# W2's loads and the remainders of W1 and W3 from GpSimd's queue, and a new order of TensorE's steps

## The chip, the cores and the metric

The kernel runs on one core of one Trainium2 chip. Its time is the device time of one execution in microseconds (us); what is told is the median of several runs. Beside it stands one execution taken by the hardware profiler, whose span (first to last instruction) and whose engines' work the profile shows.

## The reference

Two transformer layers over one sequence of 2048 positions with width 576. A layer adds memory-augmented attention on its layer norm, and then a gated feed-forward on its layer norm. Both layers use the same weights. In bf16, with 32 heads of 128, segments of 32 positions, 8 memory rows and F = 4608:

```python
for s in range(64):                                # segments, one after the other
    h = concatenate([mem, x[:, 32*s:32*s+32]])     # 8 + 32 rows of width 576
    q, k, v = h @ Wq, h @ Wk, h @ Wv               # 32 heads of 128
    p = softmax(where(mask, q @ k.T * 128**-0.5, -1e9))
    o = (p @ v) @ Wo                               # summed over the heads
    mem = o[:, :8]                                 # handed to the next segment
    outs.append(o[:, 8:])

h = silu(x @ w1) * (x @ w3)                        # 2048 x 4608
out = h @ w2

x = x + A(layernorm(x)); x = x + B(layernorm(x))   # layer 1
x = x + A(layernorm(x)); x = x + B(layernorm(x))   # layer 2
```

The memory makes the attention of a layer a chain of 64 segments. A segment of layer 2 can run as soon as layer 1 has left its group of four segments behind.

## The kernel before

**Steps.** The work goes in steps. Step t handles segment t of layer 1 and segment t-8 of layer 2 at once (`LAG = 8`), so most steps have both layers in one matmul of 80 columns: 40 rows of each. There are 72 steps; the first and last 8 have one layer alone. In a step TensorE does, by nodes of the program: `QK` and `QKt` (queries and keys of four heads, eight units; the first works on the 512 leading rows of width 576, the second on the 64-row remainder), `SC` (scores, four groups of eight heads), `PV` (P times V), `WO` and `WOt` (the output projection), and the `V` products. Softmax runs on VectorE and ScalarE: five steps on VectorE and an exponential. In steps of both layers P is transposed by a DMA, `TRD`, that reads the one buffer `PB` and writes one of two buffers `PTS`; in steps of one layer TensorE does it (`TR`).

**Feed-forward.** For each group of four segments and both layers a job runs beside the steps: layer norm (`F...`: statistics on VectorE, the reciprocal root `pow` on GpSimd, the norm on VectorE, transposes on TensorE), then 18 pairs of F blocks of 128. A pair takes W1 and W3 for 256 of the F columns and W2 for 256 of the F rows. `FF` multiplies the 512 leading rows, `FFt` the 64-row remainder, tanh and two products make the gated hidden values, and `W2` and `W2b` (one for each layer) multiply two pairs' worth by W2. The weights don't stay: every pair is loaded anew for every job.

**Buffers.** Two buffers hold W1 and W3 of a pair (pool `w13`, tile `W13`), two hold W2 (pool `w2`, tile `W2C`). So the loads of a pair wait until the pair two before has been read. A pair's load is five DMAs, all on SyncE's queue: two blocks of 128 x 4 x 256 (W1 and W3), two remainders of 64 x 256, and W2 as 128 x 2 x 576:

```python
for kind, wd in ((0, self.a.w1), (1, self.a.w3)):
    self.dma(W[:, 4 * kind:4 * kind + 4], wd[0:4 * P, fa:fa + 2 * P].rearrange("(c p) f -> p c f", p=P))
for kind, wd in ((0, self.a.w1), (1, self.a.w3)):
    self.dma(W[kind * R64:(kind + 1) * R64, 8], wd[4 * P:D, fa:fa + 2 * P])
```

**Order.** A planner places every node in the program's order. TensorE's order is not the planner's choice: it is written out by hand or by a search as a string with one letter for each TensorE node (`ORDER`: `FIRST`, then `FOUR` eleven times, then `LAST`). One `FOUR` is a round of 16 steps. The letters that matter here: Q and q are `QK` and `QKt`, S is `SC`, P is `PV`, O and o the output projection, F and f are `FF` and `FFt`, W and w are `W2` and `W2b`, a, b, m and n transposes. The other engines and the queues get their instructions in the order of the planned starts, computed from a table of durations, and each engine then works strictly in that order; waits on semaphores follow from what is read and written. Where one instruction waits, all behind it on its engine's queue wait too.

**SyncE's queue** carries the weights of the start, the five loads of each pair, the x tiles for layer 1's first norm, and the transpositions. **GpSimd's queue** carries the residual x (`XR`), the stores, the `pow` of each norm, and in each step a zeroing of `PB`, which waits until the last transposition of the step before has read it.

In the profile nearly all matmuls have line L626, VectorE's operations L632, ScalarE's L629, loads from SyncE L635, loads and stores from GpSimd L641, transpositions L1049, zeroings L1046 and `pow` L795. `W<-in_B_w_dram` are W1 and W3 (256 KB the blocks, 32 KB the remainders); the `W` in `bank<-XTB,W` is the same tile, the one in `bank<-HT,W` the weights of queries and keys.

One thing in the start depends on the order: the main part of a unit, `qk`, writes 12 matmuls of freshly loaded W against the identity ahead of units 0 and 4 of step 0, but only if it is the first to touch its banks:

```python
first = self.begin(b)
for c in range(4 if first and t == 0 and u % 4 == 0 else 0):
    for _ in range(3):
        self.mm(self.bk(b[1])[:], self.T.ident[:, 0:P], self.T.W[:, 4 + c, u * 512:(u + 1) * 512], True, True)
```

Of the kernel before, what the change touches and what calls it, by code (L numbers as in the profile page):

```python
# [199 lines left out]
def ewh(*ns):  # L200
# [2 lines left out]


FIRST = (
    "amQqQqSqQTqQQqSqQqSQqQTSvVXxPPTOPOTOoooPOoQQqqqqQSQQSvqVqQQSqTQqXPSTOPTOaooPxTOPoOoQQqqQSQqqVvSQTqqqQQSQqPSTPOOT"
    "PTOPoooOoQqqqqQQSQVvSqQQqqqQSQTPTSXPOTxOTPooPOOooQpQqqvVqqSQnQQFSqfqQQTSfqqFPQFTSOfoPWTFPOTOPfooOoFfqqQQQSFfqvVq"
    "qQWSQFQqqqfQQSTWPSFffXTFPxOTWFTfPOPOOooooFfqqQQFSQfVqqqvQWSQFffqFQTQSPWTQqfqOPSFTOPFWTOPooffOooFQQqqqqQSWQvVfSFQ"
    "qQTqWaSQPqqQTOSPboXTOPoTOPxxOooXQpqqqQQSvnQfqQSFqqQVSFffQFPqqQfFSPWOFoPfOoOofWPFOoFfqqQQQSWqqqQQQqfSFSGqgqQQFfgP"
    "GSWPFGFffggGOPOWPOOooooFfqqQQWSfqqFQQvFSVqqfQQFqfSQWQqfPaSfFPOOPWOFFPfoooOoWQqqqqQQbSQGqqgSQQQqSPGgqQOSPGOgGPgOP"  # L210
    "oooOoQqqqppQQQvSqqVnnSQFqfqQQFPSqffFQPWOSwFFPffOOwPWOooooFffqqQFQQwQSWFqfqFSGqqgfQQQPQSWFqqfgGSGPwGggOPOOPwOoooo"
    "WFqffFQQQwQqqqWSaSFqfqqQQQvSVffqFQFPPwOWSofFOFPwWffFPOOoooWQqqqQQSqqqbQQQSwGSgqqgQQPGSggGPGOPOOPoooOo"
)
FOUR = (
    "QqqqppQvVSQQnnQFfqqFSfqqQQFfqQSWPwPSFffOOWPFOFPwOooooFqffqQQQQqgqWSwGSFfqqQQQPQSWFqfqfFSGwgggGPGOPOPOOWooooFqqff"
    "QQFQQqqvwSSFfqqVQwQWFPSFffqqQQPOWSwFFPffOOWPwOooooFfqqQQqqaSQQWqqSQqqQQQbSwGSggGPGggPGOPOOPoooOo"
)
LAST = (
    "QqqppQQSQvqqqVSQQnqqnQSFPfqfQOoPSFOFPWfOFPwOoooFffqqQQQQfqqWSSwFfqqFQQwQWQqqSFffggGFPGWSwPFggfGGPOOPwOOoWoooFqfq"
    "qQQQSFqfqQQvSVqqfFQQQqfSPWwSOPFFOPWwffFPOOoWwoooFQQqfqFSqfqQQQSqqWQvVSqqQQVSPPbwXvxOPOOPoooOoQQppvqqVqqQSQQqqnnQ"  # L220
    "SFfqFTSQQPTfqfFPSWOOwFTffFTPWPOOooowoFfqvVqqQQQwQSFqqqfQSQWTSFfqfqQFQwPSTWPFTffFPOTOPOOoooowxvXVqqQQQqqQWSSFQffq"
    "qQFSQTwFTfqqQPWTSOFPFPTOfPOOoooowWqqQQQSQqqfvVSwFWffFTQPqqQWqqSQTQPOSwbOTXPxooTOPoOoQqqpQQSVqqvQQQSqqqnSQqTQFPST"
    "fOPFTOPofoTOPwOfooFVfqqvQQFSQFqqqfQQSQqqqQQSTwPTFSPOOfxooTXfPTFPOOooFQfqqqQQSVvqqwQQFSfqTQqqQSQPwTSOPFffTOFPwTOP"
    "oofOooFVvqqqQQQqSqqQQSQwQTqqSQPTSOFPFfoOTTofPPOOoopwFFffnFFwfffFFwffFfFwwwfffFFFFwffFFwffFFwffFFwfffFFww"
)
ORDER = FIRST + FOUR * 11 + LAST

# [8 lines left out]
def make_nodes(em, nseg, pools, o=Opt, dma_bw=230e3, load_bw=400e3):  # L236
# [34 lines left out]
    b = banks(1)  # L271
# [190 lines left out]
                 prio=prio, mode="full/col", acq=b, name="POST")  # L462
        return node("DVE", dve(576), em.post_add(li, g, xr[g], b[0]), deps=[d], prio=prio, rel=b, name="POSTa")

    last_up = []
    last_reads = [], []
    kept = {}

    def job(j):

        ents = [(0, j)] if 0 <= j < ngrp else []
# [6 lines left out]
        last = s0 >= nst  # L478
        wr = []
# [26 lines left out]
        for at, pp in enumerate([npp - 1] + list(range(npp - 1)) if last else range(split, npp)):  # L506
            mids, w2s, htts, lds = [], [], [], []
            stays = last and pp == npp - 1
            ents = own + [(1, own[0][1] - 1)] if last and pp == 0 else own
            ne = len(ents)  # L510
            mm = (128 * ne / 2.4 + 2.5) / 1000
            for pr_ in (2 * pp, 2 * pp + 1):
                prio = s0 + o.ff + (o.win if s0 + 4 < nst else o.last_win) * (2 * at + pr_ % 2) / NPR
                if stays:
                    w13, w2 = kept[pr_]
                    ld = []
                    w2s.append(w2)
                elif last:
                    w13 = w2 = None
                    ld = tail[pp]  # L520
                else:
                    keep = s0 < nst <= s0 + 4 and pp == npp - 1
                    w13, w2 = Slot("w13", users=2 + keep), Slot("w2", users=ne + keep)
                    kept[pr_] = w13, w2
                    ld = [node("DMA", kb(1152, 256) / dma_bw, em.load_w13(pr_, w13), prio=prio - 1, acq=[w13], lat=2.0, name="W13")]
                    lds.append(node("DMA", kb(256, 576) / dma_bw, em.load_w2(pr_, w2), prio=prio - 0.99, acq=[w2], lat=2.0, name="W2l"))
                    w2s.append(w2)
                b = banks()
                htt = Slot("htt", users=ne)
# [46 lines left out]
    for t in range(nst):  # L576
        if t % 4 == 2 and (t + 2) // 4 < ngrp:
            x_in((t + 2) // 4)
        if t == LAG:
            ht_mem[t].append(node("DVE", 0.1, em.init_mem(1, LAG), deps=[m0e] + reads_ht.get(LAG - R_HT, []), prio=LAG - 2, name="m0"))  # L580
        if role(t) == 0 or t == 0:
            vx_pair(t - role(t), t - 1 + o.vx)
        step(t)
        if t % 4 == 1 and t // 4 < ngrp:
            x_res(t // 4)
        if t % 4 == 3:
            job((t + 1) // 4 - 1)
        elif t == nst - 1:
            job(nst // 4)
# [13 lines left out]
class Emitter:  # L603
# [788 lines left out]
```

## Time and profile before

| | |
|---|---|
| median of 3 runs | 2653.09 us (2650.92 to 2656.6) |
| the profiled execution | 2660.77 us |
| its span | 2659.0 us |
| granted TensorE clock | 0.995 |
| TensorE busy | 2570.4 us (97%) |
| VectorE, ScalarE, GpSimd busy | 2019.7, 1263.2, 129.8 us |
| HBM read | 306.72 MB |

PE is TensorE's matmuls, PEld its weight loads, which run beside them; DVE is VectorE, ACT ScalarE, POOL GpSimd, SP SyncE. A q behind the name is the queue of an engine, where DMAs are issued. A group's row gives the line, engine, operation, what is written from what, the count, then the busy time, the mean in ns, and the idle time before it with what ended it. A row of waits gives who waited for whom: us in total, times, longest. A row of DMA issues gives the size and the median time from issue to landing. A row of windows gives, for a stretch, the busy time of each engine, the granted clock, the DMA engines' share and GB/s. A row of the timeline gives start, duration, engine, line and what was done.

### The profile page before, as it was taken

Reading aid. Unit: us, or ns where it says so; the run is one execution under the profiler, and the core shown is the slowest. Engines: PE = TensorE matmul, PEld = TensorE weight load, DVE = VectorE, ACT = ScalarE, POOL = GpSimd, SP = SyncE. Lnnn points to the kernel's source line nnn. Section 1 sums busy time; section 2 is a strip of 40 time slices with the busy share of each in tenths; the row PEclk is TensorE's granted clock in tenths of the full one; section 3 lists DMA queues with packets and bytes.
Section 4 is the critical chain, followed back from the end, with each engine's and each line's share of the span. In section 5 each row is a group of like instructions: output and inputs, shape, how many; then the busy total and the mean of one; then the engine's idle time right before and its main releaser. Section 6 shows DMA issues by size and latency. Waiting matters only on the chain.

```text
span 2659.0 us, 131834 instructions
## 1 busy us (share of the span) xinstructions
PE 2570.4 (97%) x58597; PEld 2216.3 (83%) x58626; DVE 2019.7 (76%) x5188; ACT 1263.2 (48%) x3694; POOL 129.8 (5%) x182
## 2 busy tenths in 40 slices
PE   6999999999999999999999999999999999999998
PEld 4787888888888888888888888888888888888886
DVE  4777776877787778778777877877777777778876
ACT  2655553544445454444545444454544445454552
POOL 1000000000000000000000000000000000000000
PEclk9999999999999999999999999999999999999999
DMA  9065745465565556556555645545465454645357
GB/s 322 8 187 129 186 101 142 122 147 137 125 144 115 145 119 157 131 126 142 113 145 118 156 131 130 147 111 140 117 157 140 122 148 101 151 114 146 108 162 240
DMA packets 683196, 371.39 MB, mean 140 GB/s; under 512 B 233752, under 2 KB 672800, under 8 KB 681984
## 3 DMA queue, kind: packets, MB, share of 16 engines
q1 hardware_dynamic: 678944, 355.00, 52.4%
q8 instruction: 458, 7.50, 1.2%
q0 software_dynamic: 3024, 6.93, 0.9%
q10 hardware_dynamic: 656, 1.02, 0.2%
q14 instruction: 114, 0.93, 0.1%
HBM read 306.72 MB, written 2.36 MB: 116 GB/s over the span
## 4 chain that ended last, share of the span: by engine, by line
PE 83%; DMA 10%; DVE 4%; issue 2%; SPq 1%; ACT 1%; POOL 0%; ACTq 0%; DVEq 0%; POOLq 0%
PE bank L626 83%; DMA PTS<-PB 6%; DMA W<-in_B_w_dram 3%; DVE PB L632 1%; SPq L635 1%; DVE SME L632 1%; DMA W<-in_A_Wk_dram 1%; DVE STAT L632 1%; DVE HTT L632 1%; DMA WO<-in_A_Wo_dram 0%; DVE V L632 0%; DMA XN<-in_A_x_dram 0%; DVE XR L632 0%; ACT HT L629 0%; ACT HTT L629 0%
## 5 line engine op out<-in xcount | busy, mean ns | idle before, releaser
L626 PEld LDWEIGHTS <-W 128*128 128x128 bf16 (+2 forms) x32200 | 1261.3, 100 | 137.2 <-issue 68.9
L626 PE MATMUL bank<-HT,W 128*128 128x80 bf16 (+3 forms) x23040 | 798.1, 197 | 13.6 <-issue 6.5
L626 PE MATMUL bank<-XTB,W 128*64 128x256 bf16 (+5 forms) x9160 | 660.5, 263 | 14.5 <-DMA W<-in_B_w_dram 11.1
L629 ACT ACTIVATE QKT<-bank 128x64 bf16<-128x64 f32 (+2 forms) x1640 | 379.5, 309 | 301.8 <-PE bank L626 269.6
L626 PE MATMUL bank<-OT,WO 128*128 128x80 bf16 (+3 forms) x11520 | 403.0, 198 | 3.3 <-issue 1.6
L626 PEld LDWEIGHTS <-WO 128*128 128x128 bf16 (+1 forms) x11520 | 377.1, 102 | 29.6 <-issue 13.1
L629 ACT ACTIVATE V<-bank 32x512 bf16<-32x512 f32 (+1 forms) x586 | 331.8, 585 | 120.5 <-PE bank L626 113.9
L626 PE MATMUL bank<-WV,HT 128*32 128x512 bf16 (+4 forms) x3572 | 360.8, 381 | 4.8 <-issue 4.0
L626 PE MATMUL bank<-W2C,HTT 128*64 128x288 bf16 (+1 forms) x3248 | 325.0, 287 | 0.4 <-DVE XR L632 0.2
L632 DVE TENSOR_TENSOR PB<-SME,STAT 40x128 bf16<-40x128 f32 (+4 forms) x912 | 275.3, 336 | 40.6 <-DMA PTS<-PB 29.6
L629 ACT ACTIVATE OT<-bank 128x320 bf16<-128x320 f32 (+1 forms) x413 | 153.3, 405 | 282.7 <-PE bank L626 276.0
L632 DVE TENSOR_REDUCE STAT<-SME 104x8 f32<-104x320 f32 (+1 forms) x576 | 275.0, 477 | 13.9 <-ACT SME L629 6.4
L629 ACT ACTIVATE HTT<-bank 128x512 bf16<-128x512 f32 (+1 forms) x322 | 174.9, 552 | 226.4 <-PE bank L626 224.7
L632 DVE SCALAR_TENSOR_TENSOR HTT<-HTT,bank 128x512 bf16<-128x512 bf16 (+1 forms) x322 | 201.3, 625 | 104.6 <-ACT HTT L629 101.4
L632 DVE SCALAR_TENSOR_TENSOR XR<-bank,XR 128x288 f32<-128x288 f32 x574 | 242.2, 450 | 38.9 <-PE bank L626 33.5
L626 PEld LDWEIGHTS <-HT 128*32 128x32 bf16 (+4 forms) x3600 | 153.5, 99 | 133.5 <-issue 27.4
L626 PEld LDWEIGHTS <-HTT 128*64 128x64 bf16 (+1 forms) x3320 | 232.2, 106 | 32.8 <-issue 3.1
L629 ACT ACTIVATE SME<-SME 104x320 f32<-104x320 f32 (+1 forms) x288 | 135.2, 469 | 209.7 <-DVE SME L632 207.7
L632 DVE TENSOR_TENSOR HTT<-HTT,bank 128x512 bf16<-128x512 bf16 (+1 forms) x322 | 203.4, 632 | 31.1 <-PE bank L626 0.9
L632 DVE CAST V<-bank 64x512 bf16<-64x512 f32 (+1 forms) x278 | 190.3, 685 | 13.6 <-PE bank L626 8.2
L632 DVE CAST QKT<-bank 128x256 bf16<-128x256 f32 (+4 forms) x408 | 111.5, 318 | 92.7 <-PE bank L626 90.2
L632 DVE TENSOR_TENSOR SME<-bank,maskb 104x320 f32<-104x320 f32 (+1 forms) x288 | 137.8, 479 | 31.9 <-PE bank L626 28.0
(59 smaller groups left out, 1331.3 us busy)
## 6 DMA issues: line engine op xcount, KB each, us to landing
W<-in_B_w_dram SPq DMA_DIRECT2D x608, 256.0 KB, 3.6
W2C<-in_B_w_dram SPq DMA_DIRECT2D x304, 288.0 KB, 3.3
W<-in_B_w_dram SPq DMA_DIRECT2D x608, 32.0 KB, 3.5
W<-in_B_w_dram SPq DMA_DIRECT2D x8, 1024.0 KB, 13.8
W<-in_A_Wq_dram SPq DMA_DIRECT2D x9, 512.0 KB, 9.8
WO<-in_A_Wo_dram SPq DMA_DIRECT2D x4, 1152.0 KB, 16.8
XR<-in_A_x_dram POOLq DMA_DIRECT2D x16, 288.0 KB, 3.6
WV<-in_B_w_dram SPq DMA_DIRECT2D x4, 1152.0 KB, 9.3
```

Of the source, the lines that this page charges most:

```text
L626: self.ch("PE", self.nc.tensor.matmul(out, lhsT=lhsT, rhs=rhs, start=start, stop=stop, skip_group_check=True, **k))
L629: self.ch("ACT", self.nc.scalar.activation(*a, **k))
L632: self.ch("DVE", getattr(self.nc.vector, fn_)(*a, **k))
L635: self.ch("SP", self.nc.sync.dma_start(out=out, in_=in_))
```

## The change

The two 64-row remainders of a pair become a node of their own, `W13t`, issued from GpSimd's queue, as W2's load is. In the plan they wait for the up-projection two pairs before. `FF` depends on the blocks alone, `FFt` on blocks and remainders. The blocks of W1 and W3 and the transpositions stay on SyncE's queue. The last job's loads, into the tiles of the attention weights, are not touched. The strings of TensorE's order have been searched anew: each has the same letters as before in another sequence.

```diff
-    "QqqqppQvVSQQnnQFfqqFSfqqQQFfqQSWPwPSFffOOWPFOFPwOooooFqffqQQQQqgqWSwGSFfqqQQQPQSWFqfqfFSGwgggGPGOPOPOOWooooFqqff"
-    "QQFQQqqvwSSFfqqVQwQWFPSFffqqQQPOWSwFFPffOOWPwOooooFfqqQQqqaSQQWqqSQqqQQQbSwGSggGPGggPGOPOOPoooOo"
+    "QqqqppQvVSQQnnQFqfqfFSFQfqqqQQSWPwSFffPOOFPFWOPwOooooFffqqQQwQQqqSWFSGfqqgQQQPQSwFqqffFSGWgggGPGOPOPOOoooowWFFqq"
+    "ffQQQWQfqqwSSQQFvqqVFSFfqfqQQPWPOSwffFPFOOwPWOooooFqfqQQqqaSQQqqWSQqqQQQSbwGSggGPGPggGOPOOPoooOo"
...
-    last_up = []
+    last_up, ups = [], []
...
                     ld = [node("DMA", kb(1152, 256) / dma_bw, em.load_w13(pr_, w13), prio=prio - 1, acq=[w13], lat=2.0, name="W13")]
-                    lds.append(node("DMA", kb(256, 576) / dma_bw, em.load_w2(pr_, w2), prio=prio - 0.99, acq=[w2], lat=2.0, name="W2l"))
+                    ldt = [node("POOL", 1.2, em.load_w13t(pr_, w13), deps=ups[-2:][:1], prio=prio - 1, acq=[w13], lat=3.5, name="W13t")]
+                    lds.append(node("POOL", 0.6, em.load_w2(pr_, w2), deps=ups[-2:][:1], prio=prio - 0.99, acq=[w2], lat=3.5, name="W2l"))
...
-                ff = node("PE", 2 * mm, em.ffn_up(ents, pr_, w13, b, last and not stays, True), deps=wr + ld, prio=prio + o.fft, mode="row",
+                ff = node("PE", 2 * mm, em.ffn_up(ents, pr_, w13, b, last and not stays, True), deps=wr + ld + ldt, prio=prio + o.fft, mode="row",
...
+                ups.append(fm)
...
+        return f
+
+    def load_w13t(self, pr, w13):
+        def f(n):
+            fa = pr * 2 * P
             for kind, wd in ((0, self.a.w1), (1, self.a.w3)):
-                self.dma(W[kind * R64:(kind + 1) * R64, 8], wd[4 * P:D, fa:fa + 2 * P])
+                self.swdma(self.T.W13[kind * R64:(kind + 1) * R64, w13.i, 8], wd[4 * P:D, fa:fa + 2 * P])
         return f
 
     def load_w2(self, pr, w2):
         fa = pr * 2 * P
-        return lambda n: self.dma(self.T.W2C[:, w2.i], self.a.w2[fa:fa + 2 * P, :].rearrange("(b p) d -> p b d", p=P))
+        return lambda n: self.swdma(self.T.W2C[:, w2.i], self.a.w2[fa:fa + 2 * P, :].rearrange("(b p) d -> p b d", p=P))
```

`FIRST` and `LAST`, the strings of the start and the end, change in the same way. `FIRST` now begins `maqqqQQS`, with remainders of three units ahead of the first main part; before it began `amQqQqSq`.

More of the change, by code (lines that the diff above doesn't have):

```diff
@@ L205 @@
 FIRST = (
[L206 to L210, printed above, removed]
@@ L211 @@
-    "oooOoQqqqppQQQvSqqVnnSQFqfqQQFPSqffFQPWOSwFFPffOOwPWOooooFffqqQFQQwQSWFqfqFSGqqgfQQQPQSWFqqfgGSGPwGggOPOOPwOoooo"
-    "WFqffFQQQwQqqqWSaSFqfqqQQQvSVffqFQFPPwOWSofFOFPwWffFPOOoooWQqqqQQSqqqbQQQSwGSgqqgQQPGSggGPGOPOOPoooOo"
+    "maqqqQQSQqQqQQqSTSQqTQqSVvxXPPTOOPTOPoooOoQQqqqqQSQQSqqvVQQSqTQqXPSTOPTOaooPxTOPoOoQQqqQSQqqvVSQTqqqQQSQqPSTPOOT"
+    "PTOPoooOoQQqqQSQqqvVSQqqQQQSqTqPSTXPOTxOTPooPOOooQqpQVqvQnSqqQFQSfqqQFTSQqfqQFTPSWPFTOffPOTOPoooOoFFqffqQQQSqVvq"
+    "qQWSQQfqfTFFQSqqQPWSFTXfxfTFPOTPOPOWOooooFfqqQQQSFqqfVvQWQSqfFTFqqfQQPSWTQfqPOSFTOPFWTOPoooffOoFQQqqqqQSWQVvSfFQ"
@@ L213 @@
+    "qQTqWqSTQPPQqOSbOoTaoPXTOPxxOooXQpQqqQSqvnqqQQSFqfQVfSFqQQqFPPSffFOWOPFfOooofFPWOoFfqqQQQSWqqqQQQqfSFSGqgfQFPQqg"
+    "GSWPGFfggfFGPOPOOOooooWFqqfqQQQSFfqQvWSFVqfqQQFfqSQQqWPSFffPOOPWFOFooPofaOoWQqqqqQQbSQQQSgqqGQPSqgGqQOSPoGGgOPgO"
+    "PooOoQqqppQQQvqqVSnnSQQFqfqfFFSQPfqqQOWPSwffFOPFWOFPwOooooFqqffQQQSFfqqWQQQSwGgqfqFPFSQQfqqgGWSwPGggOOPGFPOOoWoo"
+    "oFqffqQQQQqqwSSFqfqqQQWQwvSVfqfFQFSPWPFwaffOFOPWfwPFOOooooWQQqqqQSqqqbQQQSwGSqqggQQPGSggGPGOPOOPoooOo"
 )
 FOUR = (
-    "QqqqppQvVSQQnnQFfqqFSfqqQQFfqQSWPwPSFffOOWPFOFPwOooooFqffqQQQQqgqWSwGSFfqqQQQPQSWFqfqfFSGwgggGPGOPOPOOWooooFqqff"
@@ L216 @@
-    "QQFQQqqvwSSFfqqVQwQWFPSFffqqQQPOWSwFFPffOOWPwOooooFfqqQQqqaSQQWqqSQqqQQQbSwGSggGPGggPGOPOOPoooOo"
+    "QqqqppQvVSQQnnQFqfqfFSFQfqqqQQSWPwSFffPOOFPFWOPwOooooFffqqQQwQQqqSWFSGfqqgQQQPQSwFqqffFSGWgggGPGOPOPOOoooowWFFqq"
+    "ffQQQWQfqqwSSQQFvqqVFSFfqfqQQPWPOSwffFPFOOwPWOooooFqfqQQqqaSQQqqWSQqqQQQSbwGSggGPGPggGOPOOPoooOo"
 )
 LAST = (
-    "QqqppQQSQvqqqVSQQnqqnQSFPfqfQOoPSFOFPWfOFPwOoooFffqqQQQQfqqWSSwFfqqFQQwQWQqqSFffggGFPGWSwPFggfGGPOOPwOOoWoooFqfq"
-    "qQQQSFqfqQQvSVqqfFQQQqfSPWwSOPFFOPWwffFPOOoWwoooFQQqfqFSqfqQQQSqqWQvVSqqQQVSPPbwXvxOPOOPoooOoQQppvqqVqqQSQQqqnnQ"
@@ L221 @@
[L221 to L224, printed above, removed]
+    "QqqppQQSqQqqqvVnSQnQQfqSFqfPQOoSPFOFPwfOFPWOoooFqqffQQQFWQqqwSSFffqqQQQQqqWwSFffggGFPGSFPGfggOGPOPOOWwoooFoFffqq"
@@ new lines @@
+    "QQQQqqSvVwWSFQqqqfQQQqfSWwSPFPFOWwOPffFPOOFoWooowQQfqqFSfqqQQQSqqWQvVSqqQQVSPPbwXvxOPOOPoooOoQQppqqVvqqQSQQqnnQS"
+    "FfqqqQTQSFPTffSFFPWwOTFPffFTOOPwOooWooFqqffQQQWSwQqvVqqqQQSFSTQQqqffFSPwTWPOTFffFTPOPOOooooWxvXVqwQQqqqQQSFqfqfF"
+    "QTQSWQSqqfFPQwTSOFTPffFPTOOPwOooooWQQqqqqQSVvWQwSFffFQTqqQPWqqSQTQPOSwbOTXPxoTOPooOoQqqpQQSVvqqQQQSqqqnSQqTQFTSP"
+    "FPOTOofoPfTOPFOoowfVvqqqQQQQSfqqFSQFfqqqQQQTSwTPFSPOOffxTXPooTFPOOooFQfqqQQSwvqqVQFSQqfqQQSqqTQPwTSFPffOTOFPFTOP"
+    "ooofOowVvqqqQQqQSQQSqqQwqQSTQqPSTOffPFTFPOTOPoooOoFpwnffFFFwfffFFwfffFFwwwfffFFFFwffFFwffFFwffFFwfffFFww"
@@ L515, in job @@
                     w13, w2 = kept[pr_]
-                    ld = []
+                    ld, ldt = [], []
                     w2s.append(w2)
@@ L520, in job @@
                     ld = tail[pp]
+                    ldt = []
                 else:
```

## The prediction

> **What bounds the kernel now.** I read the busy table of the page first, then the windows by stage, the waits of each engine, the DMA issues, and at last the timeline of one stall.
>
> ```profile
> span 2659.0 us, 131834 instructions
> PE 2570.4 (97%) x58597; PEld 2216.3 (83%) x58626; DVE 2019.7 (76%) x5188; ACT 1263.2 (48%) x3694; POOL 129.8 (5%) x182
> core 0: us, PE busy (x) PEld busy (x) DVE busy (x) ACT busy (x) POOL busy (x), PEclk, DMA share, GB/s
> 0.00:250.00 250.00, 216.19 (x6206) 179.16 (x6208) 175.31 (x477) 128.39 (x363) 17.28 (x32) 0.97 0.52 160
> 250.00:2375.00 2125.00, 2086.85 (x45737) 1809.78 (x45763) 1631.81 (x4167) 1006.76 (x2978) 100.74 (x135) 1.00 0.55 135
> 2375.00:2659.00 284.00, 267.37 (x6658) 227.35 (x6657) 212.61 (x544) 128.04 (x353) 11.82 (x15) 0.98 0.52 155
> ```
>
> TensorE is the bound: it is busy 97% of the span at a granted clock near 1.00. Its idle time is 2659.0 - 2570.4 = 88.6 us: 33.8 in the start, 38.2 in the 2125 us in which both layers run, 16.6 at the end. A change of queues adds no arithmetic, so what it can win is part of the 38.2, and what it can lose is new idle time. DMA engines are busy 55% in that stage: bandwidth is not short.
>
> ```profile
> PE bank L626 <- DMA PTS<-PB: 19.6, 26, 2.3
> PE bank L626 <- DMA W<-in_B_w_dram: 11.1, 12, 2.1
> PEld L626 <- DMA W<-in_B_w_dram: 16.1, 19, 2.3
> PEld L626 <- DMA W2C<-in_B_w_dram: 1.8, 9, 0.2
> PEld L626 <- issue: 160.4, 495, 4.0
> SPq L635 <- PE bank L626: 991.3, 645, 72.9
> SPq L1049 <- DVE PB L632: 315.1, 92, 22.3
> POOL PB L1046 <- DMA PTS<-PB: 1071.0, 45, 44.0
> ```
>
> Two transfers are waited for: P's transposition (PTS, 19.6 us in 26 waits) and W1's and W3's pieces (W; 11.1 us by the matmuls, 16.1 by the weight loads ahead of them). W2 is all but hidden (1.8). SyncE's queue stands most of its time, on TensorE for a free buffer or on VectorE for a P, and whatever is queued behind waits too. GpSimd is nearly always idle, but its idle time is one long wait in order: a zeroing of PB waits up to 44.0 us for a transposition, and what comes behind it on that queue waits as well.
>
> **The loads that move.** Each of the 304 pairs of F blocks has five loads on SyncE now; two 32 KB remainders and one 288 KB block of W2 go to GpSimd, two 256 KB blocks stay.
>
> ```profile
> W<-in_B_w_dram SPq DMA_DIRECT2D x608, 256.0 KB, 3.6
> W2C<-in_B_w_dram SPq DMA_DIRECT2D x304, 288.0 KB, 3.3
> W<-in_B_w_dram SPq DMA_DIRECT2D x608, 32.0 KB, 3.5
> XR<-in_A_x_dram POOLq DMA_DIRECT2D x16, 288.0 KB, 3.6
> L641 POOL DMA_DIRECT2D XR<-in_A_x_dram x16: 572/572/722, 53.1 to 2370.4; - x16
> L641 POOL DMA_DIRECT2D out_dram<-XN x15: 552/552/594, 509.9 to 2636.3; - x15
> DMA to landing us min/median/max: 2.1/3.6/6.2
> 1320.08 2.02 SPq L1049 DMA_TRANSPOSE PTS<-PB  x1
> 1322.19 2.30 SPq L635 DMA_DIRECT2D W<-in_B_w_dram  x4
> 1327.58 0.55 PE L626 MATMUL bank<-XTB,W 64*128 64x256 bf16 x4 [1.42 <-DMA W<-in_B_w_dram]
> ```
>
> The last three rows are one of the stalls. The set of four W loads follows a transposition; the remainders are third and fourth, so they go out about 1.15 and 1.7 us after the first (half and three quarters of 2.30), and the matmuls that idle 1.42 us are the 64-row ones, which need the remainders alone. On GpSimd's queue the remainders no longer stand behind their blocks. A load from there lands as fast: 3.6 us for XR against 3.3 for W2 of the same size. So a wait on a remainder loses up to 1.15 us, more than the mean wait (16.1/19 = 0.85). The rows do not split the 19 waits into blocks and remainders; between none and all of 16.1, I take rather more than half: **-9 us**. What is late next is the block itself, which goes out no earlier than before.
>
> GpSimd's own cost: an issue takes 0.55 to 0.57 us. A remainder has 64 rows instead of 128, so at most that; W2 has 256 pieces, so between 0.57 and twice it, 1.14. That is 304 x (2 x 0.57 + 0.57 to 1.14) = 520 to 693 us, with 130 now: a quarter to a third of the span, on a queue with nothing else. What is queued behind a load there: the reciprocal root of a layer norm (64), the zeroing of PB (71), the x loads and stores. In the new instruction streams I took, for each of them, the TensorE instruction whose end the load ahead waits for, and the one from which the step itself follows. In a round of 16 steps no root has a load ahead of it that becomes free later than its own input; it loses at most the 0.3 us of a root ahead. A zeroing loses 0.7 at most (a late one would hold the next write of P and its transposition), loads of one burst about 1 us to each other. The cover of a root is the room between the transposes of the residual addition and those of the norm, 6.4 us of other matmuls in both orders. Cost: **0**, with the rival below as upper end; below nothing it can't be, since nothing leaves this queue.
>
> SyncE keeps 608 blocks and 224 transpositions. The transposition's own wait is for VectorE (315.1 us behind PB alone), so a freer queue starts few of them earlier. I count no gain for that.
>
> **The new order of TensorE.** Same steps, another sequence. Counted in the two instruction streams: 58,626 matmuls become 58,731, the columns streamed are the same but for 24 matmuls of 512 columns which vanish (below), and changes between tile shapes fall from 1,291 to 1,276. A change shows as idle weight loading put down to "issue": 160.4/1,291 = 0.12 us at least, 160.4/495 = 0.32 at most; 15 fewer are worth **-2 us** (-1.9 to -4.8).
>
> ```profile
> 1328.06 2.47 PE L626 MATMUL bank<-OT,WO 128*128 128x80 bf16 x64
> 1317.73 1.80 PE L626 MATMUL bank<-XTB,W 128*128 128x256 bf16 x16
> PTS<-PB SPq DMA_TRANSPOSE x224, 3.0
> ```
>
> With durations such as the first two rows I added up, in either order, the TensorE work that stands between a group's scores (SC) and its P.V. In that room run five VectorE steps, one exponential, the write of P and the 3.0 us transposition; the 26 waits on PTS are where it is too short. The shortest of the 224 rooms is 8.2 us in both; the one at 5% goes from 8.5 to 8.8, at 10% from 8.8 to 9.2, at 20% from 9.3 to 10.0. The 26 waits (12% of 224) are 0.75 us each on average. With 0.35 us more: 26 x 0.35 = **-9 us**, between 0 (if VectorE is late for other reasons) and -19.6.
>
> The same count speaks against the change at one place. The room between the last reader of a W1/W3 buffer and the first matmul that needs the next blocks in it was 6.5 us or more everywhere; now three up-projections stand close together once in a round, and it is 3.6 us, in 12 rounds. A block's issue takes 2.30/4 = 0.58 us and its landing 3.6, so 4.2: short by 0.6, 12 x 0.6 = **+7 us**; nothing if TensorE stands there for another reason, and +18 if each loses 1.5.
>
> **The start.** The 24 matmuls that vanish read freshly loaded W against the identity ahead of step 0 (they are written only where the main part of a QK unit comes before its remainder; the new order has the remainders first).
>
> ```profile
> 30.32 0.59 PE L626 MATMUL bank<-W,ident 128*128 128x512 bf16 x1
> 31.14 2.69 PE L626 MATMUL bank<-W,ident 128*128 128x512 bf16 x10 [0.22 <-issue]
> 25.11 1.17 PE L626 MATMUL bank<-HT,W 64*128 64x40 bf16 x40
> 29.00 1.50 PE L626 MATMUL bank<-HT,W 64*128 64x40 bf16 x40
> 23.00:26.00 3.00, 2.68 (x96) 2.43 (x92) 1.40 (x4) 0.61 (x2) 0.00 (x0) 1.00 1.03 416
> 29.00:32.00 3.00, 2.78 (x46) 1.90 (x46) 0.33 (x1) 0.74 (x2) 0.00 (x0) 0.52 1.05 426
> ```
>
> Forty QK matmuls took 1.17 us at clock 1.00 and 1.50 at 0.52. If the two units of 80 behind the lost matmuls now run at the low clock: 160/40 x 0.33 = +1.3 us. The second batch took 0.59 + 2.69 = 3.3 us; if its weights were there already, that is won. The first pair's loads from GpSimd now go out in the start, 352 KB; at 416 GB/s they hold W back by +0.8. Together **0**, from -3.3 to +2.1. The Trainium skill, TensorE: Matmul & The Clock Gate, Part 1: The HAM clock gate, says that the array stays at half clock until about 3.4 us of sustained work: by that the two units would lose up to 6.8 us of full clock, and an estimate from it is +3.4 in place of +1.3. The trace agrees in kind (0.52 after an idle stretch, 1.00 three microseconds later).
>
> **Sum.** -9 - 9 - 2 + 7 + 0 + 0 = -13 us. The profiled execution took 2660.8 us (span 2659.0 and 1.8 around it), 7.7 above the median 2653.1; I put the sum on both: 2647.8 for such an execution, **2640** as the median.
>
> **Rivals.**
> *Slower: loads from GpSimd land late.* One mechanism: with 912 more loads the software queue's landing moves from its median 3.6 to its longest, 6.2. Of 36 remainders in a round, seven have under 7.0 us of room in the new streams (5.5, 5.8, 6.0, 6.0, 6.3, 6.5, 6.9); with 0.57 for the second issue they need 6.8: the pairs lose 1.0, 0.8 and 0.3, in 12 rounds +25. The -9 on W is then not won: -9 - 2 + 7 + 25 = +21, **2674**. It decides from a landing of about 5.2 on. For it: XR has reached 6.2, and only 31 loads a run show this queue. Against: the median, and 55% DMA share. With other ways to be late on that queue (issues over 1.14 us), 0.27.
>
> *No change.* The stalls on W and P are replaced by those behind them (VectorE is busy 76%, so a P that may start earlier isn't ready earlier): only -2 + 7 are left, and half of W, -4.5: **2654**. Chance 0.12.
>
> *VectorE locks GpSimd out.*
>
> ```profile
> L632 DVE CAST V<-bank 64x512 bf16<-64x512 f32 (+1 forms) x278 | 190.3, 685 | 13.6 <-PE bank L626 8.2
> L632 DVE CAST QKT<-bank 128x256 bf16<-128x256 f32 (+4 forms) x408 | 111.5, 318 | 92.7 <-PE bank L626 90.2
> L632 DVE CAST OT<-bank 128x320 bf16<-128x320 f32 (+1 forms) x163 | 74.8, 460 | 93.3 <-PE bank L626 91.4
> ```
>
> If an issue had to wait for a cast to end: these three fill 376.6 us, 14% of the span, so of 912 issues 130 would wait, for 0.69 us at most. Of the remainders, the four tightest pairs of a round then lose 2 x 0.69 x 0.14 = 0.2 each: 4 x 12 x 0.2 = +10, so -3: **2650**. The 31 issues of the trace stay within 552 to 722 ns beside a VectorE that is busy 76% of the time, which speaks against it: 0.05. This is a rule of the Trainium skill, SBUF — State Buffer, SBUF: two separate sides: a load from GpSimd's queue can't write its descriptors while VectorE runs in a mode that takes both ports; it advises the hardware queues instead. The trace does not bear it out.
>
> That the loads don't move can be ruled out: the new streams have 912 on GpSimd.
>
> **How the numbers follow.** Forecast 0.56, late landing 0.27, no change 0.12, lock-out 0.05. A measurement of this kernel can tell some 0.2% (5.3 us) from no change. The forecast's own bounds run from -16 - 19.6 - 4.8 - 3.3 = -44 to +18 + 2 - 2 = +18, but their ends don't meet; with half of each way, as from two terms of four, it runs from about 2620 to 2660. For the range I take in the late rival's 2674. Faster: the forecast (0.52 of 0.56) and a third of no change, 0.04: 0.56. Within 0.2%: 0.04 of the forecast, 0.05 of no change, the lock-out's 0.05: 0.14. Slower: the late case, and what is left of no change: 0.30. Range 2620 to 2674.
>
> **What would show it.** Right: waits of PE and its weight loads on W fall to a third, with nothing of note on W2C; waits on PTS halve; a short wait for the 256 KB blocks once in a round; POOL at 650 to 820 us with landings of 3.3 to 4. Wrong: landings from GpSimd over 5 us, VectorE waiting for roots or zeroings on POOL, or waits on PTS above 20 us.

## The result, and the profile after

The changed kernel takes **2748.34 us** (median of 4 runs, 2740.24 to 2749.37); the kernel before took 2653.11 (2650.92 to 2656.6) beside it. The ratio is **1.0351**, with a 95% interval of 1.0328 to 1.0374: slower by 3.5%. The prediction of 2640 us, within 2620 to 2674, was wrong, in sign too.

The profile of the changed kernel, in the order in which that of before was read: the busy table, the windows by stage (the rounds end at 2450 us now), the longest waits, the DMA issues with their median landing. Line numbers have moved: matmuls are L629, VectorE L635, ScalarE L632, loads from SyncE L638, from GpSimd L644, transpositions L1057.

```profile
span 2738.5 us, 132266 instructions
PE 2585.5 (94%) x58702; PEld 2224.9 (81%) x58731; DVE 2016.7 (74%) x5104; ACT 1269.4 (46%) x3778; POOL 674.1 (25%) x1094
...
core 0: us, PE busy (x) PEld busy (x) DVE busy (x) ACT busy (x) POOL busy (x), PEclk, DMA share, GB/s
0.00:250.00 250.00, 209.68 (x6114) 175.36 (x6114) 173.25 (x471) 123.30 (x355) 55.22 (x96) 0.98 0.49 157
250.00:2450.00 2200.00, 2104.55 (x45899) 1819.61 (x45926) 1628.58 (x4091) 1016.79 (x3064) 550.25 (x888) 0.99 0.54 131
...
PE bank L629 <- DMA PTS<-PB: 53.7, 36, 3.6
PE bank L629 <- DMA W<-in_B_w_dram: 20.0, 14, 2.4
PE bank L629 <- DMA W2C<-in_B_w_dram: 9.6, 9, 3.1
SPq L1057 <- DVE PB L635: 525.2, 99, 25.4
...
W<-in_B_w_dram SPq DMA_DIRECT2D x608, 256.0 KB, 4.0
W2C<-in_B_w_dram POOLq DMA_DIRECT2D x304, 288.0 KB, 3.5
W<-in_B_w_dram POOLq DMA_DIRECT2D x608, 32.0 KB, 3.7
```

The span grew by 79.5 us. Of that, 64.4 is idle time of TensorE (2738.5 - 2585.5 = 153.0 now, 88.6 before), and 15.1 is longer busy time (2585.5 against 2570.4). In the idle time the three waits for transfers make 52.6: PTS +34.1 (53.7 against 19.6), W +8.9, W2C +9.6. The rounds hold most of it: they idle 95.5 us in 2200 (38.2 in 2125 before). GpSimd's landings are as forecast (3.5 and 3.7). SyncE waits longer for VectorE's P than before (525.2 against 315.1), so its queue is freer; the transpositions still come late.

Folding the waits on PTS by their place in the round gives the first clue. Of the 16 `PV` of a round, the third, behind the letters `SWPwSFffPOOF`, waits in each of the eleven rounds, for 1.6 to 3.6 us, 26.7 us in all; the twelfth waits 10.8 us in all; the other fourteen 5.8 together. The timeline of the changed kernel at one of the eleven, rows of SyncE, GpSimd and the matmuls that read PTS, and below it windows of that stretch:

```profile
1039.98 1.46 POOL L644 DMA_DIRECT2D W2C<-in_B_w_dram  x2 [4.16 <-PE bank L629]
1041.52 0.92 SPq L638 DMA_DIRECT2D W<-in_B_w_dram  x2
...
1042.53 2.11 POOL L644 DMA_DIRECT2D W<-in_B_w_dram  x4 [1.10 <-PE bank L629]
1043.19 1.22 SPq L1057 DMA_TRANSPOSE PTS<-PB  x1
1046.48 0.93 SPq L638 DMA_DIRECT2D W<-in_B_w_dram  x2
1050.19 0.45 PE L629 MATMUL bank<-PTS,V 128*128 128x80 bf16 x8 [3.30 <-DMA PTS<-PB]
...
1036.00:1046.00 10.00, 10.00 (x239) 9.40 (x236) 8.93 (x23) 4.64 (x15) 3.56 (x6) 1.00 0.62 155
1046.00:1051.00 5.00, 1.70 (x22) 1.42 (x20) 1.28 (x5) 0.93 (x2) 0.00 (x0) 1.00 1.02 158
1051.00:1054.60 3.60, 3.60 (x19) 2.42 (x18) 2.31 (x6) 0.11 (x1) 0.45 (x1) 0.53 0.38 87
```

Between 1040.0 and 1044.6 two loads of W2, two blocks, four remainders and the transposition go out: 1216 KB of loads (2 x 288 + 2 x 256 + 4 x 32). The transposition leaves at 1043.19, right behind the P that it moves, and lands 6.95 us later. The DMA engines are at a share of 1.02 in the 5 us in which TensorE mostly stands; the mean of 0.54 over the rounds doesn't show that. And when TensorE starts again, its granted clock is 0.53 for 3.6 us, which costs 1.7 us more, as busy time. There are eight such stretches in the changed kernel's rounds, of 3.41 or 6.83 us each, behind waits of 1.7 to 3.6 us, six of them waits on PTS; in the rounds before there is one.

### The profile page after: what moved, and what is told of

It reads as the page before. It is cut to its first block, busy times and chain, and to the rows that moved or that the text cites. A ratio compares the mean times of both kernels' runs of the same rounds, so it can differ in the third digit from the quotient of the medians.

```text
span 2738.5 us, 132266 instructions
## 1 busy us (share of the span) xinstructions
PE 2585.5 (94%) x58702; PEld 2224.9 (81%) x58731; DVE 2016.7 (74%) x5104; ACT 1269.4 (46%) x3778; POOL 674.1 (25%) x1094
## 3 DMA queue, kind: packets, MB, share of 16 engines
q10 hardware_dynamic: 656, 1.02, 0.2%
## 4 chain that ended last, share of the span: by engine, by line
PE 73%; DMA 15%; DVE 6%; issue 3%; ACT 1%; POOL 0%; SPq 0%; ACTq 0%; DVEq 0%; POOLq 0%
PE bank L629 73%; DMA PTS<-PB 11%; DMA W<-in_B_w_dram 2%; DVE PB L635 2%; DVE STAT L635 1%; DVE SME L635 1%; DMA W2C<-in_B_w_dram 1%; DVE XR L635 1%; DMA W<-in_A_Wk_dram 1%; DVE HTT L635 1%; DMA WV<-in_A_Wv_dram 0%; DVE V L635 0%; SPq L638 0%; DMA XN<-in_A_x_dram 0%; ACT V L632 0%
## 5 line engine op out<-in xcount | busy, mean ns | idle before, releaser
L629 PEld LDWEIGHTS <-W 128*128 128x128 bf16 (+2 forms) x32232 | 1264.8, 101 | 172.0 <-issue 87.7
L629 PE MATMUL bank<-HT,W 128*128 128x80 bf16 (+3 forms) x23040 | 801.5, 197 | 27.1 <-DMA W<-in_A_Wk_dram 9.1
L629 PE MATMUL bank<-XTB,W 128*64 128x256 bf16 (+5 forms) x9192 | 670.8, 266 | 22.8 <-DMA W<-in_B_w_dram 20.0
L632 ACT ACTIVATE QKT<-bank 128x64 bf16<-128x64 f32 (+4 forms) x1716 | 393.8, 312 | 314.9 <-PE bank L629 300.2
L644 POOL DMA_DIRECT2D W<-in_B_w_dram x608 | 321.9, 535 | 666.1 <-PE bank L629 661.4
L629 PE MATMUL bank<-OT,WO 128*128 128x80 bf16 (+3 forms) x11520 | 401.4, 198 | 1.6 <-issue 1.1
L629 PEld LDWEIGHTS <-WO 128*128 128x128 bf16 (+1 forms) x11520 | 378.0, 102 | 21.4 <-issue 5.8
L632 ACT ACTIVATE V<-bank 32x512 bf16<-32x512 f32 (+1 forms) x563 | 321.2, 586 | 119.1 <-PE bank L629 110.1
L629 PE MATMUL bank<-WV,HT 128*32 128x512 bf16 (+4 forms) x3571 | 362.2, 384 | 6.4 <-issue 4.2
L644 POOL DMA_DIRECT2D W2C<-in_B_w_dram x304 | 222.9, 735 | 546.2 <-PE bank L629 539.3
L635 DVE TENSOR_TENSOR PB<-SME,STAT 40x128 bf16<-40x128 f32 (+4 forms) x912 | 275.7, 336 | 88.0 <-DMA PTS<-PB 79.5
L629 PE MATMUL bank<-W2C,HTT 128*64 128x288 bf16 (+1 forms) x3456 | 328.9, 289 | 9.8 <-DMA W2C<-in_B_w_dram 9.6
L632 ACT ACTIVATE HTT<-bank 128x512 bf16<-128x512 f32 (+1 forms) x322 | 174.3, 553 | 296.4 <-PE bank L629 295.3
L635 DVE TENSOR_REDUCE STAT<-SME 104x8 f32<-104x320 f32 (+1 forms) x576 | 275.5, 478 | 20.3 <-ACT SME L632 12.7
L632 ACT ACTIVATE OT<-bank 128x320 bf16<-128x320 f32 (+1 forms) x417 | 154.7, 406 | 286.2 <-PE bank L629 272.0
L635 DVE SCALAR_TENSOR_TENSOR XR<-bank,XR 128x288 f32<-128x288 f32 x574 | 243.4, 449 | 59.5 <-PE bank L629 54.2
L635 DVE SCALAR_TENSOR_TENSOR HTT<-HTT,bank 128x512 bf16<-128x512 bf16 (+1 forms) x322 | 200.7, 623 | 110.5 <-ACT HTT L632 108.2
L629 PEld LDWEIGHTS <-HTT 128*64 128x64 bf16 (+1 forms) x3528 | 238.4, 107 | 44.4 <-DMA W2C<-in_B_w_dram 6.8
L629 PEld LDWEIGHTS <-HT 128*32 128x32 bf16 (+4 forms) x3600 | 151.3, 99 | 142.2 <-issue 36.8
L632 ACT ACTIVATE SME<-SME 104x320 f32<-104x320 f32 (+1 forms) x288 | 135.5, 470 | 206.1 <-DVE SME L635 203.9
L635 DVE TENSOR_TENSOR HTT<-HTT,bank 128x512 bf16<-128x512 bf16 (+1 forms) x322 | 203.4, 632 | 30.3 <-DVE HTT L635 1.4
L635 DVE CAST V<-bank 64x512 bf16<-64x512 f32 (+1 forms) x301 | 206.1, 685 | 19.7 <-PE bank L629 13.0
```

Of the source, the lines that this page charges most:

```text
L629: self.ch("PE", self.nc.tensor.matmul(out, lhsT=lhsT, rhs=rhs, start=start, stop=stop, skip_group_check=True, **k))
L632: self.ch("ACT", self.nc.scalar.activation(*a, **k))
L635: self.ch("DVE", getattr(self.nc.vector, fn_)(*a, **k))
L644: self.ch("POOL", self.nc.gpsimd.dma_start(out=out, in_=in_))
```

## The experiments

Two theories. **A:** the transpositions are held up by loads in flight. For the first four runs it said that the loads from GpSimd's queue alone do this and that the order is harmless; after them it was widened to loads on any queue, of which the queues and the order together put more in the way. **B:** the new sequence itself leaves too little between scores and P.V, whatever the loads do. The runs were made on three chips, four kernels on each, and each group beside the kernel before on the same chip: 2640.32 us for the first four, 2653.82 for the second, 2655.31 for the third. Ratios, not times, are compared across groups.

**The order alone**: the kernel before with the new strings.

```diff
-FIRST, FOUR, LAST of before
+FIRST, FOUR, LAST of the change
```

> The new order of TensorE's steps, all loads on SyncE's queue as before. Theory A (the loads from GpSimd's queue make transpositions and blocks land later): the order is harmless, 2640 to 2665 us, transpositions land in 3.0 us as before and TensorE's waits on them stay near 20 us. Theory B (the new order itself leaves too little room, at the three up-projections that stand close together above all): nearly the whole loss is here, 2720 to 2750 us, with 50 us of waits on transpositions.

2751.33 us, ratio **1.0401** (1.0385 to 1.0418). That is the loss that B gave, even a little more, and not A's: on the old queues the new order costs the whole loss. But the waits are not of B's kind. Its waits on PTS are the longest of all runs, though its transpositions land fast (median 2.8 us). The rows of SyncE, of VectorE's writes of P and of P.V at one stall:

```profile
PE bank L626 <- DMA PTS<-PB: 76.3, 53, 4.1
PTS<-PB SPq DMA_TRANSPOSE x224, 2.8
...
1289.16 6.59 SPq L635 DMA_DIRECT2D W<-in_B_w_dram  x8
1291.38 1.12 DVE L632 TENSOR_TENSOR PB<-SME,STAT 40x128 bf16<-40x128 f32 x4
1295.85 5.42 SPq L1049 DMA_TRANSPOSE PTS<-PB  x2
1298.61 0.71 PE L626 MATMUL bank<-PTS,V 128*128 128x80 bf16 x8 [2.55 <-DMA PTS<-PB]
```

P is written at 1292.5, but SyncE stands at a set of eight W loads until 1295.75, so the transposition goes out 3.3 us late. On the old queue the new order has another fault: loads that wait for TensorE stand ahead of a finished P. Of the 53 waits, 32 with 56.0 of the 76.3 us are on transpositions that leave over 1 us after P is written; in the changed kernel none of the 36 is.

**The queues alone**: the changed program with the old strings.

```diff
-FIRST, FOUR, LAST of the change
+FIRST, FOUR, LAST of before
```

> The loads on GpSimd's queue, the order of before. Theory A: nearly the whole loss, 2710 to 2750 us, transpositions landing in 3.3 us instead of 3.0 and waits on them of 40 us or more. Theory B: 2640 to 2665 us with waits on transpositions near 20 us.

2694.3 us, ratio **1.0187** (1.0161 to 1.0213). Neither theory had that: A gave 2710 us or more, B 2665 at most. So neither the order nor the queues are all of it. Beside PTS, a wait stands here for HTT, the gated hidden values, that the kernel before has once (0.2 us) and the changed kernel not at all:

```profile
PE bank L629 <- DMA PTS<-PB: 26.4, 28, 3.3
PE bank L629 <- DVE HTT L635: 15.9, 12, 1.6
```

It is 1.3 us on average, about once in a round. The other engines' sequences are planned from the loads' durations too, and the new ones make VectorE take the gated product later.

**One half of the queues each**, with the old strings.

```diff
+W2 from GpSimd, the remainders from SyncE          (first run)
+the remainders from GpSimd, W2 from SyncE          (second run)
```

> W2's loads alone on GpSimd's queue, remainders back on SyncE's, the order of before. Theory A with the bytes as cause (W2 is 288 of 352 KB that move): four fifths of what queues_alone loses, some 2715 us. Theory A with the number of loads as cause (304 of 912): a third, some 2680 us. Theory B: 2640 to 2665 us.

> The remainders alone on GpSimd's queue, W2 back on SyncE's, the order of before. Theory A by bytes: a fifth of the loss, some 2670 us; by the number of loads: two thirds, some 2705 us. Theory B: 2640 to 2665 us.

W2 alone: 2664.66 us, **1.0073** (1.0047 to 1.0098). The remainders alone: 2639.99, **0.9996** (0.9981 to 1.0010). Both are below what A gave, and at or near what B had; the waits on PTS are 13.6 and 18.8 us, no more than the 19.6 of the profile before, so one half alone does not hold the transpositions up further. The halves add up to 0.7%, both together cost 1.9; each of these runs has a plan of its own, and the difference was not taken apart. With the remainders alone the waits on W went, as the prediction has them:

```profile
PE bank L629 <- DMA W<-in_B_w_dram: 1.3, 2, 0.9
PEld L629 <- DMA W<-in_B_w_dram: 2.3, 4, 1.4
```

All 12 matmul waits on W in the profile before were on 64-row matmuls, the readers of remainders. Yet the time did not move. In the profile of W2 alone, on the same chip, where the remainders are still on SyncE, 7.5 us of such waits stand, so little more could be won there; the interval of 0.9996 leaves room for 5 us.

**The queues with the plan of before untouched**: every engine keeps its sequence, and only the issuing queue of the two kinds of load differs.

```diff
-self.dma(W[kind * R64:(kind + 1) * R64, 8], ...)
+self.swdma(W[kind * R64:(kind + 1) * R64, 8], ...)
-return lambda n: self.dma(self.T.W2C[:, w2.i], ...)
+return lambda n: self.swdma(self.T.W2C[:, w2.i], ...)
```

> The kernel before, with its plan untouched (the sequences of TensorE, VectorE and ScalarE and the places of all loads in it), in which W2's loads and the remainders are issued on GpSimd's queue in place of SyncE's. The run of the new queues with the old strings took 1.0187 of the kernel before; in it TensorE waited 1.4 us for a product HTT of VectorE once in each round (15.9 us), because VectorE's sequence had been planned anew. Theory A (what the queues themselves cost is loads in flight beside the transpositions): these 15.9 us go, the waits on PTS stay at 20 to 35 us: 1.008 to 1.013 of the kernel before. Theory C (GpSimd's loads land too late for W2 or the remainders whatever the plan): the same 1.019 or more, with waits on W2C of 8 us or more.

2679.39 us, **1.0089** (1.0068 to 1.0110): within theory A's band. The waits on HTT are gone (0.2 us), those on W nearly (1.2):

```profile
PE bank L626 <- DMA PTS<-PB: 33.7, 36, 2.6
PE bank L626 <- DMA W2C<-in_B_w_dram: 7.9, 9, 1.6
```

So of the 1.9%, about half is the queues themselves and half the plan made anew, in which the waits on HTT are 15.9 us. The two runs were on different chips.

**One stretch of the order put back.** The third `PV` of the round again, 19 letters of `FOUR`, the same steps in the old sequence:

```diff
-SWPwSFffPOOFPFWOPwO
+SWPwPSFffOOWPFOFPwO
```

> The changed kernel with one stretch of 19 letters of FOUR, around the third P of a round, put back as it was before (the same multiset of steps; eleven rounds). In the changed kernel this one P waits 1.6 to 3.6 us for its transposition in each of the eleven rounds, 26.7 of the 53.7 us of waits on PTS; there the transposition goes out 0.5 to 2.6 us after two 256 KB blocks and up to four remainders, and lands in 5.2 to 7.9 us. Theory A (loads in flight make the transposition late; the order put them ahead of it): the blocks now go out behind the transposition, which lands in under 5 us, the 26.7 us go, and with them the half-clock stretches behind about six of the eleven waits (1.7 to 3.4 us each, some 12 us): about 2710 us, PTS waits 25 to 30 us in all. Theory B (the new sequence as a whole leaves too little work between scores and P.V, and the loss only shows at this place): the waits move to the next P, and the time stays within 10 us of the changed kernel's.

2715.08 us, **1.0245** (1.0221 to 1.0270): 19 letters hold 1.1 of the 3.5% (1.0351 - 1.0245), some 28 us. The same place in this kernel's timeline:

```profile
1041.50 1.23 SPq L1057 DMA_TRANSPOSE PTS<-PB  x1
1042.82 1.09 SPq L638 DMA_DIRECT2D W<-in_B_w_dram  x2
1043.24 2.11 POOL L644 DMA_DIRECT2D W<-in_B_w_dram  x4 [2.76 <-PE bank L629]
1046.38 0.45 PE L629 MATMUL bank<-PTS,V 128*128 128x80 bf16 x8
```

The transposition leaves ahead of the blocks and the remainders, and P.V starts without a wait. As A has it, the third `PV` loses nothing any more (26.7 us before). But the second one now waits 13.8 us in the eleven rounds, so the waits on PTS fall only to 40.9, not to the 25 to 30 expected. Its transpositions land in 2.7 to 4.4 us, no later than at the same place of the changed kernel (2.6 to 4.5), where it does not wait: the swap puts this P.V ahead of S, F, f and f, so here the room is short, as B has it.

**All loads on GpSimd**, so that SyncE's queue holds nearly only transpositions.

```diff
-self.dma(W[:, 4 * kind:4 * kind + 4], ...)
+self.swdma(W[:, 4 * kind:4 * kind + 4], ...)
```

> The changed kernel, order kept, with the two 256 KB blocks of W1 and W3 on GpSimd's queue too, so that SyncE's queue holds nearly only transpositions. Theory A1 (a transposition is late because it stands behind the blocks of its own queue): it lands in 2.6 to 3.3 us nearly everywhere, waits on PTS fall from 53.7 to under 20 us, and the time to about 2700 us, less what blocks behind remainders on GpSimd cost. Theory A2 (all queues share the same 16 DMA engines, and what counts is the bytes in flight): it still lands in 5 us or more at the third P of the round, waits on PTS stay at 40 to 60 us, 2740 us or more. Theory B (the sequence itself): 2740 us or more with landings near 3 us and waits for VectorE or for PTS all the same.

2842.43 us, **1.0711** (1.0685 to 1.0736). The DMA issue row of the transposition and the two longest waits for transfers:

```profile
PTS<-PB SPq DMA_TRANSPOSE x224, 4.1
PE bank L629 <- DMA PTS<-PB: 63.4, 41, 4.7
PE bank L629 <- DMA W<-in_B_w_dram: 54.5, 46, 2.9
```

A queue of its own does not help: the transposition lands in 4.1 us in the median (3.3 in the changed kernel), and there are 41 waits with 63.4 us (36 with 53.7). A1 falls. At the third `PV` of the round the transposition still lands in 5.3 us or more in eight of the nine rounds that can be read, as A2 has it, though P.V hardly waits there now (0.2 us); it waits at the fourth, the fifth and the twelfth. Not all of the 7.1% is the queue: the plan was made anew, and TensorE waits 17.6 us on HTT, as it does not in the changed kernel. The Trainium skill, DMA: Bandwidth & Descriptors, Issuing engines are not separate DMA queues, says that transfers started by different engines run on the same 16 DMA engines and interleave, and that another issuer saves only issue time. This run agrees: loads that left the transposition's queue still delay it.

**Thin loads**: fewer bytes, all issues and the order as in the changed kernel.

```diff
-self.swdma(self.T.W2C[:, w2.i], w2[fa:fa + 2 * P, :])        # first run
+self.swdma(self.T.W2C[:, w2.i, :, 0:64], w2[fa:fa + 2 * P, 0:64])
-self.swdma(W13[..., 8], wd[4 * P:D, fa:fa + 2 * P])          # second run
+self.swdma(W13[..., 8, 0:32], wd[4 * P:D, fa:fa + 32])
```

> The changed kernel, in which each load of W2 after the first into a buffer brings 64 of the 576 columns: as many pieces and issues, a ninth of the bytes (32 KB in place of 288). The rest of W2 is left out and old data are used for it. Theory A2 (bytes in flight): the transposition of the third P of the round lands in about 4 to 5.5 us in place of 5.2 to 7.9, waits on PTS fall from 53.7 to 25 to 40 us, and the time to about 2715 us. Theory A1 (the blocks ahead in its own queue): waits on PTS stay at 45 to 55 us; only the 9.6 us on W2 go: about 2735 us. Theory B: no change but those 9.6 us.

> The changed kernel, in which each remainder after the first into a buffer brings 32 of its 256 columns: as many pieces and issues, an eighth of the bytes (4 KB in place of 32). The rest of the remainders is left out and old data are used for it. Theory A2 (bytes in flight): four remainders are 128 of some 900 KB in flight around the late transposition, so 0.5 to 1 us of its landing: waits on PTS 40 to 48 us, the time about 2735 us. Theory A1: no change (2740 to 2750). If the number of pieces from the second queue, not their bytes, holds the transposition up: no change either.

Thin W2: 2695.03 us, **1.0163** (1.0143 to 1.0183). Thin remainders: 2729.21, **1.0274** (1.0245 to 1.0304). The first, with its busy table:

```profile
PE 2570.4 (95%) x58702; PEld 2216.2 (82%) x58731; DVE 2016.2 (75%) x5104; ACT 1268.9 (47%) x3778; POOL 672.8 (25%) x1094
PE bank L630 <- DMA PTS<-PB: 33.5, 34, 3.7
PE bank L630 <- DMA W2C<-in_B_w_dram: 2.5, 3, 1.7
```

W2's bytes carry over half of the loss (1.9 of the 3.5%, 50 us): 20.2 of waits on PTS, 7.1 on W2C, and 15.1 of TensorE's busy time, which is back at 2570.4: three half-clock stretches are left in the rounds, of eight. The waits on PTS are where A2 had them; at the third `PV` 15.2 of 26.7 us stay, with landings of 4.3 to 6.2 us. The time is 20 us lower than A2 had (2715), and those 15.1, which it had not counted, are most of that. Cutting the remainders to an eighth of their bytes saves 20 us (1.0351 - 1.0274), a little more than expected; the remainder still lands in 3.5 us (3.7), and the waits on PTS are 45.9, as A2 had them.

**All loads thin**, in the changed kernel and in the kernel before.

```diff
-blocks 128 x 4 x 256, remainders 64 x 256, W2 128 x 2 x 576
+blocks 128 x 1 x 256, remainders 8 x 256, W2 128 x 1 x 256
```

> The changed kernel with nearly no load traffic in the rounds: after the first load of each block pair, a block brings 128 of its 512 rows, a remainder 8 of its 64, W2 128 rows of 256 columns in place of 256 rows of 576. The rest is left out, and old data are used. Order, issues and waits stay. Theory A (the loss is loads in flight beside transpositions): waits on PTS under 10 us, on W and W2C under 5, the clock at 1.00 in the rounds, the time 2635 to 2660 us. Theory B (the new sequence leaves TensorE too little work between scores and P.V, whatever the loads do): waits on PTS 30 us or more, 2700 us or more.

> The kernel before, with the same parts of the loads left out as in the run of the changed kernel with thin loads. Waits on PTS (19.6) and W (11.1) nearly vanish: 2615 to 2630 us. The difference between the two thin runs is what the new sequence costs by itself: under 25 us by theory A, of which the start is 5; over 60 us by theory B.

The changed kernel: 2634.32 us, **0.9922** (0.9903 to 0.9941). The kernel before: 2627.1, **0.9896** (0.9870 to 0.9922). The waits on PTS of the one and of the other:

```profile
PE bank L630 <- DMA PTS<-PB: 14.0, 19, 1.9
```

```profile
PE bank L627 <- DMA PTS<-PB: 14.5, 22, 1.4
```

For the loss as a whole this settles A against B. With little load traffic the two kernels are 7 us apart, of which the start may be 4 (below). The traffic left out cost the kernel before 28 us (2655.3 - 2627.1) and the changed kernel 114 ((1.0351 - 0.9922) x 2655). The new sequence with little traffic is about as good as the old; it is what it does to the traffic that is dear.

The waits on PTS do not vanish, though: 14.0 us is above the 10 that A had at most, and in the kernel before 14.5 of 19.6 stay. So the loads account for most of what the change added, but not for most of the waits that were there before; what makes those is open. The landings say the same. In the changed kernel they take 3.0 us on average where other packets fill less than a tenth of the DMA engines' time from 1.2 to 4 us behind the issue (67 transpositions), and 4.9 where they fill 0.5 to 0.7 of it (34). In the kernel before it is 3.4 (68) and 4.0 (14), with 3.1 in between, at 0.3 to 0.5 (72).

**The old start**: the first 53 letters of `FIRST` put back.

```diff
-maqqqQQSQqQqQQqSTSQqTQqSVvxXPPTOOPTOPoooOoQQqqqqQSQQS
+amQqQqSqQTqQQqSqQqSQqQTSvVXxPPTOPOTOoooPOoQQqqqqQSQQS
```

> The changed kernel with the first 53 letters of FIRST put back as they were before (main part of QK ahead of its remainder, with the 24 matmuls against the identity; P.V and its transpositions in the old places); all else as in the changed kernel. If the start's own sequence costs what the profiles show (the first masked scores of step 1 at 60.8 us before, 65.0 after): they are back at 61 to 62 us, and the time is 3 to 6 us under the changed kernel's (ratio 1.033 in place of 1.035). If the 352 KB from GpSimd's queue in the start cost it: still 64 to 65 us, and no gain.

2734.4 us, **1.0299** (1.0268 to 1.0329). VectorE's first masked scores of step 1 in the kernel before, the changed kernel and this one:

```profile
60.83 0.48 DVE L632 TENSOR_TENSOR SME<-bank,maskb 40x320 f32<-40x320 f32 x1
```

```profile
65.02 0.48 DVE L635 TENSOR_TENSOR SME<-bank,maskb 40x320 f32<-40x320 f32 x1
```

```profile
61.58 0.48 DVE L635 TENSOR_TENSOR SME<-bank,maskb 40x320 f32<-40x320 f32 x1
```

So the new start costs 4.2 us, of which 3.4 are its sequence; the 352 KB from GpSimd cost 0.75 at most. The time fell by 0.5%, 14 us, more than 3.4; the interval reaches down to 6 us (1.0351 - 1.0329, with the changed kernel's own uncertainty beside it), and the profile shows the rest only as shorter waits in the rounds, on W (13.6 us for 20.0) and W2C (5.6 for 9.6). That remainder stays open.

## Why the prediction was wrong, step by step

**What bounds the kernel**: TensorE, right. "DMA engines are busy 55% in that stage: bandwidth is not short" is where the error begins. The share is 0.54 after the change as well, but 1.02 in the stretch that was shown.

**The waits on remainders, -9**: right in kind. All 12 waits of the matmuls were for remainders, one of them, of 0.35 us, for a load of the last job that does not move; so the term could have been 10.8. The 16.1 that it was taken from are the weight loads' side of the same stalls. In the changed kernel no matmul waits for a remainder, but the run with the remainders alone was not faster for it.

**The tight place, +7**: right place and kind, mis-sized. Once in each of 12 rounds a matmul of the 512 leading rows waits for its block behind the three up-projections, 18.6 us in all, just past the end of +18 given there. The landing of a block had been taken at its median of 3.6; there it takes 4.4 to 5.7 us.

**More room for the transposition, -9: the step that failed.** It took the 26 waits as a lack of TensorE work between scores and P.V and gave them 0.35 us more of it, with the landing fixed at its median of 3.0. But in the 21 waits of the profile before that can be matched to the landing of one transposition, it goes out 0.08 us after P is written and lands in 4.3 us on average, while all of them take 3.3; in 28 of the changed kernel, 0.07 and 5.5, with 3.8 for all. The landing is no constant, and the change moved loads into the way, which made it longer: of the 53.7 us of waits, all but 14.0 go when the loads are thin. The term was +34.1 in waits and most of the +15.1 of clock, where -9 had been forecast. Whether more room would have won anything of the 19.6 us with the loads left where they were, no run shows.

**W2, nothing of note**: wrong by 9.6 us; the run with the plan untouched has 7.9 too, so this belongs to the queues. **Shapes, -2**: too small to be seen. **The start, 0**: +4 up to step 1, most of it by the sequence of the first step, which the term did not look at. **GpSimd's own queue, 0**: right: busy 674 us, in the 650 to 820 given; an issue takes 0.52 for a remainder and 0.74 for W2, VectorE waits for a root five times, 3.8 us in all, and for a zeroing never. A root takes 0.55 us or more in the profile before, not the 0.3 that the term had; that changed nothing.

**The rivals.** The late rival had the sign, but not the mechanism: landings from GpSimd stayed at 3.5 to 3.7 in the median, far from the 5.2 at which it decides, and no matmul waited for a remainder. What came late was another queue's transfer beside them. The lock-out does not show in the issues: at most 0.77 us for a remainder. That none of the rivals let one queue's loads delay another queue's transfer is why 2674 was too low an end.

The sum as it should have stood, from these runs: the queues +0.9% (the plan untouched), the plan made anew +1.0%, the new order on these queues +1.6% (1.0351 - 1.0187); putting back the stretch around the third `PV` of the round wins 1.1%. The parts were measured on different chips, and they add up in this sequence only: on the old queues the same order costs 4.0%.

## What to carry to other kernels

A short transfer on the critical path is priced by what is in flight when it is issued, on every queue, not by its median landing or by a mean DMA share: look at the share in the few microseconds of the stall. A second queue can let more loads start at once, which is good for the loads and bad for whatever is waited for beside them: with the plan untouched the waits on PTS were 33.7 us for 19.6, though with W2 alone moved they were 13.6. A cheap order is one in which the urgent transfer leaves first. To tell sequence from traffic, cut the bytes and keep the issues: two such runs separated the two here, for the loss as a whole.

## What was not expected of the hardware

**Behind waits of 2 us the clock is often halved.** Over the profiles of all 14 kernels, between 250 and 2375 us, I counted waits of TensorE and whether the granted clock dipped within 5 us behind them: 16 of 366 waits of 0.5 to 1.5 us and 4 of 66 of 1.5 to 2.0 us, but 22 of 47 of 2.0 to 2.5 us, 21 of 27 of 2.5 to 3.0, and 16 of 18 above. A dip lasts 3.41 us (59 of them) or 6.83 (9) at half clock, which is 1.7 or 3.4 us lost on top of the wait. The Trainium skill, TensorE: Matmul & The Clock Gate, Part 1: The HAM clock gate, puts the fall to half clock after an idle window of some 3.4 us; here waits of 2 us already have even odds.

**A quarter of the DMA engines' time goes to few bytes.** In the changed kernel with all loads thin, over 250 to 2375 us:

```profile
250.00:2375.00 2125.00, 2098.65 (x46441) 1827.09 (x46467) 1643.70 (x4132) 1027.12 (x3099) 496.78 (x892) 1.00 0.27 55
```

Half of the changed kernel's DMA share in the rounds (0.54 at 131 GB/s) is left at 55 GB/s, in a kernel that has as many transpositions and 200 of each pair's 864 KB of weights. GB/s says little about how busy the engines are here. The packets of the trace tell what takes that time: each transposition moves its 224 KB in 896 packets of 256 bytes, and packets of that size take 0.14 of the 0.27, at 24 GB/s.
